# Cross-covariance attention and a mixture of adapters: z and logits in one product, norms of k from products of k with itself

## The chip, the core and the metric

The kernel runs on one core of a Trainium2 chip. A core has TensorE (PE, matrix products, with its weight loads shown as PEld), VectorE (DVE), ScalarE (ACT), GpSimd (POOL) and SyncE (SP, which here only issues transfers), an on-chip memory of 128 partitions, a smaller memory that products are written to (PSUM, in banks of 2 KB for each partition), and 16 DMA engines that the queues of SP, ACT and POOL share. The metric is the device time of one execution in microseconds (us), the median over runs.

## The reference

q, k and v are float32 of shape (4, 6400, 256): 4 batches of 6400 rows and 256 channels. The output has 25600 rows of 256.

```python
qn = q / (norm(q, axis=1) + 1e-06)            # norms over the 6400 rows, for each channel
kn = k / (norm(k, axis=1) + 1e-06)
s = kn.transpose(0, 2, 1) @ qn / tau          # 256 x 256 for each batch
a = exp(s - s.max(-1)); a /= a.sum(-1) + 1e-09
x = v @ a                                     # 6400 x 256 for each batch
logits = x @ w_gate                           # 8 experts
# the two largest of 8 are kept, their softmax is w; for each kept expert e of a row:
out = x + sum_e w_e * ((x @ A[e]) @ B[e])     # A[e] is 256 x 16, B[e] is 16 x 256
```

## The kernel before

Rows are dealt so that a partition holds 50 consecutive rows of a batch. A *chunk* is one row from each partition, 128 rows; a batch has 50 chunks, or 25 *pairs*. A *unit* is two pairs (the last of a batch is one pair).

**Loads.** GpSimd's queue loads q, k and v and casts them to bf16 on the way (`load_more`). q and k share a tile of 10 chunks, with 4 such buffers; v comes in tiles of 18, 16 and 16 chunks, with 3 buffers. The first 4 chunks of q and k come in float32 over SP's queue into a staging tile and are cast by VectorE and ScalarE, and SP also loads the three small weights `ast`, `wst`, `bst`. The order of the loads is a list sorted by due times, moved by `LEAD`.

**First half of a batch.** `gram` (L331) adds k^T q over the 50 chunks in the bank `acc`. `square` (L308 on VectorE, L311 on ScalarE) squares pieces of up to 4 chunks of q and k, `add_squares` (L320, VectorE) adds halves of a piece, and `norm` (L345) sums over partitions by products with a column of ones into `nrm`. Then comes a chain of small steps `chain0` to `chain6`: logarithm and exponential for the root (L357, L359), reciprocal, the scaling of `acc` (L375), a product that spreads the q norms over partitions (L384), the exponential with its row sums (L396), transposes (L409) and products of the transposed matrix with `w_gate` (L426) and A (L428), which give `wa_sb`: 8 columns for the logits and 128 for z, so that v alone is multiplied.

**Second half.** For each unit, `transposes` (L493) turns v around on TensorE and ScalarE or VectorE copies it out (L500, L503). `logits` (L521) makes the logits of 10 pairs in one bank; `gating` copies them (L546) and works out the gates in a dozen small VectorE operations (L551 to L592). `z_gz` (L625) makes z in one of two banks (four at the end) and VectorE gates it directly from there into `gz` (L629). `gz_t` (L641) transposes gz into the same bank, a copy gives `gzT` (L646, L649). `y_mm` (L658) makes v a, `delta` (L667) adds gzT times B in the same bank, and ScalarE (L679, few by VectorE) copies the sum into the tile `ys`, of which there are 7, each for 5 pairs. A full tile goes out over ScalarE's queue (`send`, L694); the last 5 pairs go out one by one over SP's queue (L684).

**What sets the order.** The program is written out by a planner in the kernel's own Python: a loop `while nd < NPT` keeps an estimated clock for each engine and for the DMA, lists what TensorE could do next (Gram, norm, transposes, logits, z, gz transposes, y, delta, the chain) with the time at which it could begin, and takes the first that is ready by a fixed order of preference. The other engines' instructions are written out at the same time. The estimates shape only the order; each engine then runs its instructions in that order and waits for what they need. Stores are held back while the planner thinks that the DMA has more than `BACKLOG` us to do, unless too few `ys` tiles are left. Batch 0's small constants are built by VectorE (`constants`) and TensorE (`constant_a`, L275) at chunks 16 and 30 of the first Gram matrix.

Of the kernel before, what the change touches and what calls it, by code (L numbers as in the profile page):

```python
# [8 lines left out]
FP32 = mybir.dt.float32  # L9
# [7 lines left out]
def kernel(  # L17
# [30 lines left out]
    GATE = 10  # L48
# [4 lines left out]
    YB = 7  # L53
    VTB = 10
    FIRST = 4
    LEAD = [0.0, 0.1, -0.2, 0.2]
    BACKLOG = 4.0
# [3 lines left out]
    if VT[-1] > 10:  # L61
        V_PARTS[B - 1, len(VT) - 1] = [VT[-1] - 6, 6]
# [58 lines left out]
    sq_pool = ctx.enter_context(tc.tile_pool(name="sqp", bufs=4))  # L121
    s2_pool = ctx.enter_context(tc.tile_pool(name="s2p", bufs=4))
# [5 lines left out]
    work = ctx.enter_context(tc.tile_pool(name="work", bufs=3))  # L128
    ps_acc = ctx.enter_context(tc.tile_pool(name="psacc", bufs=1, space=bass.MemoryType.PSUM))
# [29 lines left out]
    def load_more(limit=1000):  # L159

        while limit and loads:
            pick = None
            for x in loads[:6]:
                kind = x[1]
                if x[0] > loads[0][0] + 0.25:
                    break
# [13 lines left out]
            left[kind].append(3 * size if kind == "qk" else size)  # L180
# [43 lines left out]
    transfer("store", 2 * FIRST * CHUNK + 0.5, 1.9)  # L224
# [18 lines left out]
    load_more(3)  # L243

# [41 lines left out]
    for b in range(B):  # L286
        pieces[b] = []
        for i, n in enumerate(QKT):
            sizes = ([FIRST] if (b, i) == (0, 0) else []) + (FIRST_PARTS.get(i, [n]) if b == 0 else [n])
            o = qk_c0[i]  # L290
            for m in sizes:
                for w in range(2):
                    pieces[b] += [(w, o + x, min(4, m - x)) for x in range(0, m, 4)]
                o += m

# [27 lines left out]
    squared, added = [], []  # L323

    def gram(b, c):
        if c == 0:
            acc[b] = ps_acc.tile([P, CC, C], FP32, tag="acc", name="acc")
        s, o = qk_at[c]
        t = tiles["qk"][b, s]
        for ic in range(CC):  # L330
            nc.tensor.matmul(  # L331
                acc[b][:, ic, :], t[:, 1, o, ic * P:(ic + 1) * P], t[:, 0, o, :],
                start=(c == 0 and ic == 0), stop=(c == NC - 1), skip_group_check=True)
        st.setdefault(b, {})["acc_end"] = end = run("pe", 0.22)
        used("qk", b, c, 1, end)

    def norm():
        b, i, s2, _ = added.pop(0)
        w, c, n = pieces[b][i]
        if i == 0:  # L340
            nrm[b] = ps_nrm.tile([P, 512], FP32, tag="nrm", name="nrm")
        for x in range(n // 2):
            for ic in range(CC):
                j = w * CC + ic
                nc.tensor.matmul(  # L345
                    nrm[b][:, j:j + 1], s2[:, x, ic * P:(ic + 1) * P], ones_bf[:, 0:1],
                    start=(i == 0 and x == 0 and ic == 0), stop=(i >= len(pieces[b]) - 2),
                    skip_group_check=True)
        st.setdefault(b, {})["nrm_end"] = run("pe", 0.035 * n)
        if i == len(pieces[b]) - 1:  # L350
            st[b]["normed"] = NC

    def chain0(b):
        d = st.setdefault(b, {})
        lnn = bat.tile([P, 4], FP32, name="lnn")
        norms = nrm[b][:, 0:4]
        nc.scalar.activation(lnn, norms, ACT.Ln)  # L357
        rt = bat.tile([P, 4], FP32, name="rt")
        nc.scalar.activation(rt, lnn, ACT.Exp, scale=0.5)  # L359
        d["rt"] = rt  # L360
        d["at"] = run("act", 0.4, d["nrm_end"])
# [19 lines left out]
    def chain2(b):  # L381
        d = st[b]
        bc = nrm[b][:, 256:512]
# [5 lines left out]
        d["at"] = run("dve", 0.75, run("pe", 0.45, d["at"]), d["tk_end"])  # L389
# [64 lines left out]
    for b in range(B):  # L454
        f = 0
        for n in [5, 5, 5, 5, 3, 2] if b == B - 1 else [GRP] * (NPAIR // GRP):
            g = {"b": b, "f": b * NPAIR + f, "n": n}
# [4 lines left out]
        while f < NPAIR:  # L462
            n = min(GATE, NPAIR - f)
# [14 lines left out]
    pt_end = [0.0, 0.0]  # L478

    def transposes(u):  # L480
# [25 lines left out]
        r["g"]["vT_end"] = end  # L506
        pt_end.append(end)

    def quicker(act, dve):
        return "act" if clock["act"] + act < clock["dve"] + dve else "dve"  # L510

    def logits(gr):

        n, b = 2 * gr["n"], gr["b"]
        lp = ps_t.tile([P, 512], FP32, tag="pt", name="lp")[:, 0:n * E].rearrange(
            "p (s e) -> p s e", s=n)
        i = 0
        for u in range(gr["u0"], gr["u1"]):
            for sc in range(2 * units[u]["n"]):
                for ic in range(CC):  # L520
                    nc.tensor.matmul(lp[:, i, :], units[u]["vT"][:, ic, sc, :], st[b]["wa"][:, ic, 0:E],  # L521
                                     start=(i == 0 and ic == 0), stop=(i == n - 1 and ic == 1),
                                     skip_group_check=True)
                i += 1
        gr["lp"] = lp
        gr["lp_end"] = run("pe", 0.055 * n, gr["vT_end"])

    def gating(gr):
# [15 lines left out]
        def op_lg():  # L544
            d["lg"] = t3("lg")
            V.tensor_copy(d["lg"], gr["lp"])  # L546
# [359 lines left out]
```

## Time and profile before

| | |
|---|---|
| median of 3 runs | 255.96 us (255.96 to 256.38) |
| the profiled execution | 256.35 us |
| its span, first to last instruction | 254.6 us |
| mean granted TensorE clock | 0.932 |
| busy: PE, DVE, ACT, POOL | 216.3, 169.2, 174.5, 32.3 us |
| read from HBM, written | 78.91 MB, 26.21 MB |

A row of a group names the line, the engine and the operation, what is written and read with its shape, and how often it ran; behind the bar stand its busy time in all and the mean of one in ns, then the time that the engine idled before it and what ended that. Rows of the chain and of the timeline begin with the start and the duration in us. Matrix products overlap, so the mean of one is longer than the distance from one to the next; the chain's rows, which give a run of products and its length, show the distance. For a DMA queue a row gives packets, MB as written, and the share of the 16 engines' time. The window rows give for a stretch the busy time and count of PE, PEld, DVE, ACT and POOL, then the granted clock, the DMA share and the GB/s moved; a DMA share can pass 1, since transfers overlap.

### The profile page before, as it was taken

The numbers are of one execution on the slowest core, as the hardware profiler recorded it, in microseconds if no ns is written. First come the engines' busy times: TensorE is split into PE (matmuls) and PEld (weight loads), VectorE is DVE, ScalarE is ACT, GpSimd is POOL, SyncE is SP. The second block draws the span as 40 slices with busy tenths as digits, with TensorE's granted clock in tenths as the row PEclk, the third lists the DMA queues.
The fourth block names the chain that finished last, engine by engine and source line by source line (L and its number), as shares of the span: only waits on it lengthen the run. The fifth ranks groups of instructions, "written<-read, shape, count | busy, mean of one in ns | idle before, by whom it ended". The sixth has DMA issues, their size and how long they took to land.

```text
span 254.6 us, 6828 instructions
## 1 busy us (share of the span) xinstructions
PE 216.3 (85%) x2872; PEld 189.5 (74%) x2872; DVE 169.2 (66%) x476; ACT 174.5 (69%) x279; POOL 32.3 (13%) x66
## 2 busy tenths in 40 slices
PE   0758977678999999999799946599999999999990
PEld 0445766467999989998699934389899999789980
DVE  1468554546867888788777644738879786967650
ACT  2745666648888999777796566917969866565750
POOL 8031241110111110101101000120001000000000
PEclk9999995587999999999999995779999999999996
DMA  7999999999999999999999999999999999999995
GB/s 211 228 213 216 207 213 216 217 210 218 215 216 217 213 220 208 220 212 253 321 273 264 315 314 267 215 214 213 234 299 290 269 303 320 390 427 419 416 383 220
DMA packets 12558, 66.76 MB, mean 262 GB/s; under 512 B 1520, under 2 KB 2032, under 8 KB 8816
## 3 DMA queue, kind: packets, MB, share of 16 engines
q0 software_dynamic: 8352, 38.80, 74.6%
q10 hardware_dynamic: 2736, 24.90, 23.6%
q1 hardware_dynamic: 1440, 2.63, 3.0%
q8 instruction: 22, 0.36, 0.5%
q14 instruction: 8, 0.07, 0.1%
HBM read 78.91 MB, written 26.21 MB: 413 GB/s over the span
## 4 chain that ended last, share of the span: by engine, by line
DMA 61%; PE 27%; ACT 3%; issue 2%; DVE 2%; POOL 1%; ACTq 1%; DVEq 0%; POOLq 0%
DMA qk<-in_k_dram 50%; DMA vt<-in_v_dram 11%; PE acc L331 8%; PE y_ps L658 7%; PE y_ps L667 3%; PE zg L625 3%; PE vT_ps L493 1%; PE zg L641 1%; PE nrm L345 1%; ACT ys L679 1%; ACTq L694 1%; DVE s L320 1%; POOL qk L191 1%; ACT vT L500 1%; PE A_ps L275 1%
## 5 line engine op out<-in xcount | busy, mean ns | idle before, releaser
L311 ACT ACTIVATE sq<-qk 128x1024 bf16<-128x1024 bf16 (+1 forms) x105 | 89.7, 900 | 22.2 <-DMA qk<-in_k_dram 10.7
L331 PE MATMUL acc<-qk 128*128 128x256 bf16 x400 | 66.8, 321 | 17.1 <-DMA qk<-in_k_dram 10.4
L679 ACT COPY ys<-y_ps 128x512 f32<-128x512 f32 x96 | 54.6, 586 | 20.8 <-PE y_ps L667 20.1
L331 PEld LDWEIGHTS <-qk 128*128 128x128 bf16 x400 | 41.7, 112 | 27.8 <-DMA qk<-in_k_dram 12.2
L658 PE MATMUL y_ps<-a_bf,vT 128*128 128x256 bf16 x400 | 59.3, 274 | 1.0 <-ACT ys L679 1.0
L320 DVE TENSOR_TENSOR s<-sq 128x512 bf16<-128x512 bf16 (+1 forms) x120 | 40.6, 375 | 9.5 <-ACT sq L311 5.7
L629 DVE TENSOR_TENSOR gz<-zg,gate 128x512 bf16<-128x512 f32 (+1 forms) x52 | 34.1, 669 | 15.4 <-PE zg L625 14.9
L658 PEld LDWEIGHTS <-vT 128*128 128x128 bf16 x400 | 36.4, 98 | 5.1 <-issue 1.6
L667 PE MATMUL y_ps<-ball_sb,gzT 128*128 128x256 bf16 x200 | 36.0, 272 | 0.6 <-ACT gzT L646 0.6
L493 PE MATMUL vT_ps<-ident,vt 128*128 128x128 bf16 x400 | 30.5, 224 | 2.2 <-DMA vt<-in_v_dram 1.1
L625 PE MATMUL zg<-wa_sb,vT 128*128 128x128 bf16 x400 | 30.3, 223 | 0.0
L345 PEld LDWEIGHTS <-s 128*128 128x128 bf16 x400 | 21.3, 101 | 12.0 <-DVE s L320 8.3
L500 ACT COPY vT<-vT_ps 128x1024 bf16<-128x1024 bf16 (+1 forms) x19 | 18.5, 991 | 17.0 <-PE vT_ps L493 16.7
L345 PE MATMUL nrm<-ones_bf,s 128*128 128x1 bf16 x400 | 22.9, 166 | 7.9 <-DVE s L320 6.6
L493 PEld LDWEIGHTS <-vt 128*128 128x128 bf16 x400 | 25.4, 100 | 4.0 <-DMA vt<-in_v_dram 3.0
L503 DVE COPY vT<-vT_ps 128x1024 bf16<-128x1024 bf16 (+1 forms) x33 | 21.7, 664 | 8.4 <-PE vT_ps L493 7.9
L625 PEld LDWEIGHTS <-vT 128*128 128x128 bf16 x400 | 25.9, 100 | 0.8
L191 POOL DMA_DIRECT2D qk<-in_q_dram x22 | 12.2, 556 | 94.1 <-ACT sq L311 35.8
L649 DVE COPY gzT<-zg 128x512 bf16<-128x512 bf16 (+1 forms) x40 | 16.4, 415 | 7.2 <-PE zg L641 6.5
L667 PEld LDWEIGHTS <-gzT 128*128 128x128 bf16 x200 | 18.0, 97 | 2.9 <-ACT gzT L646 0.9
L641 PE MATMUL zg<-ident,gz 128*128 128x128 bf16 x200 | 19.5, 219 | 0.7 <-DVE gz L629 0.7
L308 DVE TENSOR_TENSOR sq<-qk 128x1024 bf16<-128x1024 bf16 (+1 forms) x15 | 9.7, 654 | 13.0 <-DMA qk<-in_k_dram 7.0
(65 smaller groups left out, 158.3 us busy)
## 6 DMA issues: line engine op xcount, KB each, us to landing
out_dram<-ys ACTq DMA_DIRECT2D x19, 1280.0 KB, 12.2
qk<-in_q_dram POOLq DMA_DIRECT2D x18, 640.0 KB, 25.7
qk<-in_k_dram POOLq DMA_DIRECT2D x18, 640.0 KB, 27.0
vt<-in_v_dram POOLq DMA_DIRECT2D x7, 1024.0 KB, 30.0
vt<-in_v_dram POOLq DMA_DIRECT2D x3, 1152.0 KB, 33.0
vt<-in_v_dram POOLq DMA_DIRECT2D x2, 640.0 KB, 18.6
out_dram<-ys SPq DMA_DIRECT2D x5, 256.0 KB, 4.6
stage<-in_q_dram SPq DMA_DIRECT2D x1, 512.0 KB, 3.8
```

Of the source, the lines that this page charges most:

```text
L311: nc.scalar.activation(sq, x, ACT.Square)
L320: nc.vector.tensor_tensor(out=s2, in0=sq[:, 0:n, :], in1=sq[:, n:2 * n, :], op=OP.add)
L331: nc.tensor.matmul(acc[b][:, ic, :], t[:, 1, o, ic * P:(ic + 1) * P], t[:, 0, o, :], start=(c == 0 and ic == 0), stop=(c == NC - 1), skip_ ...
L345: nc.tensor.matmul(nrm[b][:, j:j + 1], s2[:, x, ic * P:(ic + 1) * P], ones_bf[:, 0:1], start=(i == 0 and x == 0 and ic == 0), stop=(i >= l ...
L493: nc.tensor.matmul(pt[:, ic, sc, :], vt[:, o, ic * P:(ic + 1) * P], ident, is_transpose=True, start=(i == 0), stop=(i == 2 * nch - 1))
L503: nc.vector.tensor_copy(vT, pt)
L625: nc.tensor.matmul(z[:, sc, :], r["vT"][:, ic, sc, :], st[b]["wa"][:, ic, E:E + ER], start=(sc == 0 and ic == 0), stop=(sc == nch - 1 and ...
L629: nc.vector.tensor_tensor(out=gz.rearrange("p c (e r) -> p c e r", e=E), in0=z.rearrange("p c (e r) -> p c e r", e=E), in1=gr["gate"][:, r ...
L641: nc.tensor.matmul(gt[:, sc, :], r["gz"][:, sc, :], ident, is_transpose=True, start=(sc == 0), stop=(sc == nch - 1))
L658: nc.tensor.matmul(y[:, sc, :], r["vT"][:, ic, 2 * x + sc, :], st[r["b"]]["a"][:, ic, :], start=(sc == 0 and ic == 0), stop=False, skip_gr ...
L667: nc.tensor.matmul(y[:, sc, :], r["gzT"][:, 2 * x + sc, :], ball_sb, start=False, stop=(sc == 1), skip_group_check=True)
L679: nc.scalar.copy(dst, y)
```

## The change

1. **z and logits.** `logits` and `z_gz` are gone. `z_mm` multiplies a unit's transposed v by all 136 columns of `wa_sb` into a pair of banks `zp` and copies the result to an on-chip tile `zs` (ScalarE or VectorE, whichever the planner thinks earlier). `gating` reads the logits there; `gate_z` gates z from there, on VectorE, or on GpSimd once the planner has issued every load. `gz_t` now writes to a bank of its own: the one for transposes of v, or at the end the two of `acc` and `nrm`.
2. **Norms.** `SQ` says which of q (0) and k (1) are still squared. In batch 0 neither is, in batches 1 to 3 only q. For the others `gram` multiplies each block of 128 channels by itself and adds that in `nrm`; `chain0` takes the diagonal with the identity.
3. **Small weights** are loaded over GpSimd's queue behind the first q and k loads, no longer over SP's.
4. **Stores.** The last 5 pairs share a `ys` tile and go out as 3, 1 and 1 pairs. There are 6 `ys` tiles.
5. **The planner**: other gate groups (10, 10, 5 as before for 25 pairs, now written out), other due times and estimates, `BACKLOG` 9 for 4, and another order of preference between z, transposes and the rest.

```diff
-    YB = 7
+    YB = 6
     VTB = 10
+    ZSB = 2
     FIRST = 4
-    LEAD = [0.0, 0.1, -0.2, 0.2]
-    BACKLOG = 4.0
+    GATES = [10, 10, 5]
+    GATE = max(GATES)
+    TAIL = [3, 1, 1]
+    SQ = [(), (0,), (0,), (0,)]
+    LEAD = [0.0, 0.15, 0.2, 0.2]
+    BACKLOG = 9.0
...
-    ps_z = ctx.enter_context(tc.tile_pool(name="psz", bufs=2, space=bass.MemoryType.PSUM))
+    ps_z = ctx.enter_context(tc.tile_pool(name="psz", bufs=1, space=bass.MemoryType.PSUM))
...
-    nc.sync.dma_start(ast, moe_A.rearrange("e (g j) r -> (e g) j r", j=2 * E))
-    nc.sync.dma_start(wst, moe_w_gate.rearrange("(p cc) e -> p (cc e)", p=P))
-    nc.sync.dma_start(bst, moe_B.rearrange("e r d -> (e r) d"))
...
     make_identity(nc, ident_f)
     load_more(3)
+    nc.gpsimd.dma_start(wst, moe_w_gate.rearrange("(p cc) e -> p (cc e)", p=P))
+    nc.gpsimd.dma_start(bst, moe_B.rearrange("e r d -> (e r) d"))
+    nc.gpsimd.dma_start(ast, moe_A.rearrange("e (g j) r -> (e g) j r", j=2 * E))
...
     def gram(b, c):
...
-        for ic in range(CC):
-            nc.tensor.matmul(
-                acc[b][:, ic, :], t[:, 1, o, ic * P:(ic + 1) * P], t[:, 0, o, :],
-                start=(c == 0 and ic == 0), stop=(c == NC - 1), skip_group_check=True)
+        for j in range(2 * CC):
+            w, ic = divmod(j, CC)
+            x = t[:, w, o, ic * P:(ic + 1) * P]
+            if w not in SQ[b]:
+                nc.tensor.matmul(nrm[b][:, j, :], x, x, start=b not in begun,
+                                 stop=(c == NC - 1), skip_group_check=True)
+                begun.add(b)
+            if w == 1:
+                nc.tensor.matmul(acc[b][:, ic, :], x, t[:, 0, o, :], start=(c == 0 and ic == 0),
+                                 stop=(c == NC - 1), skip_group_check=True)
...
     def chain0(b):
...
+            nc.vector.tensor_tensor(out=own[:, 0:n, :], in0=nrm[b][:, j:j + n, :],
+                                    in1=ident_f.unsqueeze(1).to_broadcast([P, n, P]), op=OP.mult)
+            nc.vector.tensor_reduce(out=ss[:, j:j + n], in_=own[:, 0:n, :], axis=AX.X, op=OP.add)
...
+    def z_mm(u):
...
+        zp = ps_z.tile([P, 2, 512], FP32, tag="zp", name="zp")
+        for x in range(r["n"]):
+            z = zp[:, x, 0:2 * (E + ER)].rearrange("p (s d) -> p s d", s=2)
+            for sc in range(2):
+                for ic in range(CC):
+                    nc.tensor.matmul(z[:, sc, :], r["vT"][:, ic, 2 * x + sc, :], st[b]["wa"][:, ic, :],
+                                     start=(sc == 0 and ic == 0), stop=(sc == 1 and ic == 1),
+                                     skip_group_check=True)
...
+        if quicker(0.16 + 0.114 * nch, 0.14 + 0.142 * nch) == "act":
+            nc.scalar.copy(dst, src)
...
+            nc.vector.tensor_copy(dst, src)
...
+    def gate_z(u):
...
+        eng = "pool" if 1 and not loads else "dve"
+        (nc.gpsimd if eng == "pool" else nc.vector).tensor_tensor(
             out=gz.rearrange("p c (e r) -> p c e r", e=E),
...
-        gt = r["zg"].bitcast(BF16)[:, 0:512].rearrange("p (s d) -> p s d", s=4)[:, 0:nch, :]
+        if free_from[0] is None:
+            full = ps_t.tile([P, 512], FP32, tag="pt", name="gzT_ps")
+        elif u % 2:
+            full = ps_acc.tile([P, 512], FP32, tag="acc", name="gzT_ps")
+        else:
+            full = ps_nrm.tile([P, 512], FP32, tag="nrm", name="gzT_ps")
...
+        eng = nc.sync if gr["f"] >= NPT - GRP else nc.scalar
+        eng.dma_start(out_v[gr["b"], :, c0:c0 + n, :], gr["blk"]["ys"][:, w:w + n, :])
```

More of the change, by code (lines that the diff above doesn't have):

```diff
@@ L291 @@
             for m in sizes:
-                for w in range(2):
+                for w in SQ[b]:
                     pieces[b] += [(w, o + x, min(4, m - x)) for x in range(0, m, 4)]
                 o += m
+    squared, added = [], []
     def piece_lands(b, i):
@@ L321, in add_squares, with norm @@
         added.append((b, i, s2, run("dve", 0.12 + 0.13 * n, end)))
-    squared, added = [], []
+    begun = set()
+    def norm():
+        b, i, s2, _ = added.pop(0)
+        w, c, n = pieces[b][i]
+        if b not in nrm:
+            nrm[b] = ps_nrm.tile([P, 2 * CC, P], FP32, tag="nrm", name="nrm")
+        for x in range(n // 2):
+            for ic in range(CC):
+                nc.tensor.matmul(
+                    nrm[b][:, w * CC + ic, 0:1], s2[:, x, ic * P:(ic + 1) * P], ones_bf[:, 0:1],
+                    start=b not in begun, stop=(c + n == NC and x == n // 2 - 1), skip_group_check=True)
+                begun.add(b)
+        st.setdefault(b, {})["nrm_end"] = run("pe", 0.035 * n)
+        if i == len(pieces[b]) - 1:
+            st[b]["normed"] = True
     def gram(b, c):
@@ L335, in gram @@
-        used("qk", b, c, 1, end)
[L337 to L351, printed above, removed]
@@ L461 @@
         f = 0
[L462 to L463 removed]
+        for n in GATES:
             g = {"b": b, "f": b * NPAIR + f, "n": n, "ready": False, "u0": len(units)}
@@ L505, in transposes @@
         r["vT"], r["vT_end"] = vT, end
-        r["g"]["vT_end"] = end
         pt_end.append(end)
[L509 to L526, printed above, removed]
     def gating(gr):
@@ L791 @@
                      [pt_end[-2], min(clock["act"], clock["dve"]) - slack])
-            t_cand = (at if ok else 1e9, "t")
-            pairs.insert(len(pairs) if nt - nz >= AHEAD_T else max(0, len(pairs) - 1), t_cand)
+            more.append((at if ok else 1e9, "t"))
+        gated = sum(u < NU and units[u]["g"]["ready"] for u in range(ng, ng + 3))
+        pairs = more + pairs if gated < 3 else pairs + more
         g_cand = []
         if added:
+            b = added[0][0]
             at = added[0][3]
-            if added[0][1] == 0 and added[0][0] > 0 and chain_at[added[0][0] - 1] < 3:
-                at = 1e9
+            if b and b not in begun:
+                at = max(at, st[b - 1].get("bc_end", 1e9))
             g_cand.append((at, "norm"))
```

225 lines of the change are left out of this document (122 added, 103 removed).

## The prediction

> **What bounds the kernel now.** I read the page first, then the DMA queues in two stretches of 10 us, then the windows at both ends, and last the chain in order of time. The page gives the load of the queues and the busiest engine:
>
> ```profile
> span 254.6 us, 6828 instructions
> PE 216.3 (85%) x2872; PEld 189.5 (74%) x2872; DVE 169.2 (66%) x476; ACT 174.5 (69%) x279; POOL 32.3 (13%) x66
> ...
> q0 software_dynamic: 8352, 38.80, 74.6%
> q10 hardware_dynamic: 2736, 24.90, 23.6%
> q1 hardware_dynamic: 1440, 2.63, 3.0%
> ```
>
> The DMA view of 70 to 80 us (loads alone) and of 230 to 240 us (stores alone) gives the rate of each kind:
>
> ```profile
> q0 software_dynamic: 464, 2.12, 104.4%
> ...
> q10 hardware_dynamic: 461, 4.20, 99.7%
> ```
>
> Loads count as bf16 here, which is half of what is read. At 2.12 MB in 10 us the 38.80 MB take 183.0 us; at 4.20 MB the 24.90 MB of stores take 59.3 us and SP's 2.63 MB 6.3 us. Together 248.6 us of transfers in a span of 254.6. The windows show where the other 6 us are (columns: stretch, length, then busy us and count of PE, PEld, DVE, ACT, POOL; granted clock, DMA share, GB/s):
>
> ```profile
> 0.00:1.00 1.00, 0.00 (x0) 0.00 (x0) 0.19 (x3) 0.26 (x1) 0.21 (x4) 1.00 0.00 0
> 1.00:2.00 1.00, 0.00 (x0) 0.00 (x0) 0.04 (x2) 1.00 (x1) 0.76 (x2) 1.00 0.40 45
> 2.00:3.00 1.00, 0.00 (x0) 0.00 (x0) 0.00 (x0) 0.02 (x1) 1.00 (x3) 1.00 0.65 172
> ...
> 45.00:50.00 5.00, 2.75 (x16) 1.97 (x17) 3.20 (x10) 3.60 (x5) 0.98 (x2) 0.50 1.06 220
> ...
> 150.00:155.00 5.00, 0.77 (x11) 0.58 (x12) 1.02 (x4) 1.34 (x3) 0.00 (x0) 0.67 1.02 320
> ...
> 240.00:245.00 5.00, 5.00 (x60) 4.62 (x59) 2.79 (x7) 2.88 (x6) 0.00 (x0) 1.00 0.90 374
> 245.00:250.00 5.00, 2.99 (x30) 2.23 (x27) 1.45 (x4) 2.58 (x5) 0.00 (x0) 1.00 0.97 395
> 250.00:254.60 4.60, 0.00 (x0) 0.00 (x0) 0.00 (x0) 0.00 (x0) 0.00 (x0) 0.57 0.43 163
> 252.00:253.00 1.00, 0.00 (x0) 0.00 (x0) 0.00 (x0) 0.00 (x0) 0.00 (x0) 0.50 0.28 109
> ```
>
> The first 3 us move 0.22 MB, worth 0.5 us: 2.5 us are lost there. 2.5 + 248.6 = 251.1, and the wire runs dry near 252.6. So the wire is the bound, and at most 252.6 - 251.1 = 1.5 us can be won on it. The same comes from the rows of the end: 374 and 395 GB/s beside 420 cost 0.55 + 0.30 us, and the slow drain after 250 us some 0.6. TensorE is no bound before the end: it idles in 150 to 155 us. But behind the last Gram matrix it sets the pace, so both nearly meet:
>
> ```profile
> 28.32 1.73 PE A_ps L275 x16
> ...
> 168.94 26.33 DMA qk<-in_k_dram
> ...
> 197.36 0.46 PE acc L331 x4
> ...
> 199.81 0.08 PE nrm L345 x4
> ...
> 205.04 0.45 PE vT_ps L493 x8
> 205.48 0.49 PE nrm L384 x2
> ...
> 214.75 1.00 PE lp L521 x40
> ...
> 227.03 0.45 PE zg L625 x8
> 227.48 0.44 PE y_ps L658 x4
> ...
> 228.57 0.22 PE zg L641 x4
> ...
> 229.68 0.44 PE y_ps L667 x4
> ...
> 248.23 0.23 PE y_ps L667 x2
> 248.49 0.59 ACT ys L679
> ```
>
> From the last Gram product (197.8) to the last delta (248.5) are 50.7 us; from there to the end of the span 6.1 (copy, SP's issue, landing, the program's end).
>
> **The change part by part.** *TensorE.* By these rows one logits product costs 25 ns, one norm product 20, one of 128 columns 56, one of 256 columns 110. Removed: 400 x 25 = 10.0 us of logits, 250 x 20 = 5.0 of norms. Added: 500 products of q or k with itself, 500 x 56 = 28.0, and 8 more columns on 400 z products, 1.4. Net +14.4 us, but not at the end. The order of the instructions puts behind the last Gram product, before: 100 transposes of v, 144 z, 100 logits, 76 gz transposes, 156 y, 80 deltas, 16 norms and the chain, 47.2 us, which took 50.7 (1.07 each). After: 100, 100 (at 59 ns), none, 64, 156, 80 and the chain: 41.6 us, with 1.07 44.6. This end gets 6 us shorter.
>
> *In front of it.* From the weights `wa` of batch 0 to the last Gram product the sum of the same counts rises from 123.6 to 133.7 us. Before, that stretch ran from 44.9 to 197.8 us with waits for data in it, such as the two windows above. After, it starts later, see below, and at 1.07 needs 143 us: from 50 to 54 that is 193 to 197. The data bound (the last k landed at 195.3) stands where it stood, since the loads behind it are the same; one y buffer less (6 for 7) makes one block of 1.31 MB go out earlier, 3.1 us on the wire ahead of it. I take the last Gram at 195 to 201, 198 for the sum, so TensorE ends at 198 + 44.6 = 242.6 where 248.5 would still be harmless.
>
> *Weights by GpSimd's queue.* The three small loads leave SP and stand behind eight q and k loads; each issue waits for an earlier landing, as POOL's rows do:
>
> ```profile
> 16.76 0.54 POOL L192 DMA_DIRECT2D qk<-in_k_dram  x1 [1.49 <-DMA qk<-in_k_dram]
> ...
> 192.38 1.06 POOL L195 DMA_DIRECT2D vt<-in_v_dram  x2 [12.02 <-PE y_ps L667]
> ```
>
> Ahead of them go 72 chunks of 65.5 KB, 4.7 MB at 212 GB/s = 22.3 us, and the staged 1 MB, 2.5: they land at about 28.5 us. VectorE then builds the constants (8 x 0.35 us and some 1.4 of small ones), so that `A_ps`, at 28.32 before, comes near 33 to 35, with 20 chunks of Gram and norm products (8.9 us, up to twice that at the clock of 0.50 that idling brought at 45 us) behind it on the same queue. Price: 6 to 10 us of delay in batch 0. It is hidden by the 57 us that TensorE does not work before the last Gram (197.8 less 141.0 of counted work) and by the loads queued: those that need no tile of these 20 chunks are 2 x 70 chunks of q and k and 34 of v, 11.4 MB, 54 us of wire, so that the next ones are wanted at about 58 us, while the tiles come free at 40 to 47. If that cover is gone it costs its full length, the second rival. The rest of the start is bounded by -0.3 us (less on SP's queue beside the staged chunks) and +0.3 us.
>
> *ScalarE and VectorE.* These rows are by shape:
>
> ```profile
> L311 ACT ACTIVATE sq<-qk 128x1024 bf16<-128x1024 bf16 x67 | 69.2, 1056 | 18.7 <-DMA qk<-in_k_dram 10.7 <-DMA qk<-in_q_dram 5.0 <-DVE s L320 3.0
> L679 ACT COPY ys<-y_ps 128x512 f32<-128x512 f32 x96 | 54.6, 586 | 20.8 <-PE y_ps L667 20.1
> ...
> L629 DVE TENSOR_TENSOR gz<-zg,gate 128x512 bf16<-128x512 f32 x48 | 32.5, 689 | 14.5 <-PE zg L625 13.9
> L320 DVE TENSOR_TENSOR s<-sq 128x512 bf16<-128x512 bf16 x80 | 31.8, 419 | 7.8 <-ACT sq L311 5.3 <-PE nrm L345 2.2
> ...
> L576 DVE TENSOR_TENSOR e<-lm,m 128x160 f32<-128x160 f32 (+1 forms) x12 | 3.5, 291 | 0.0
> ...
> masks.py:199 POOL TENSOR_SCALAR_AFFINE_SELECT ident<-ident 128x128 bf16<-128x128 bf16 x1 | 0.3, 289 | 0.1
> ```
>
> ScalarE loses 39 large squares (41 us) and more small ones, and gains 33 copies of z at about 0.62 us (by the y copy, 544 for 512 elements): 20 us, so it ends lighter. VectorE loses 50 large sums (21 us), 21 gatings (14 us) and the logits' copies and gains 19 z copies of about 0.73 us. Neither is a bound, 0 us. The diagonal of the norm products adds three small VectorE operations to each chain, some 1.2 us; in return the chain no longer waits for squares: before, 7.7 us lay between the last Gram and the chain's product (205.48); now about 3. I count 0 for it, -4 to +1.2 as ends, since other work fills TensorE meanwhile.
>
> *Gating by GpSimd.* All 21 products stand behind the last load issue (192.4 us), so no load waits for them. No run shows such a product on GpSimd; VectorE's 0.69 us is the lower bound, four times the select on 128 elements, 1.16 us, the nearest row of that engine, and twice that for its two inputs, 2.3, the upper. I take 1.16: 24 us in about 50, while TensorE has 3.6 us of work for each. 0 us; at 2.3, 48 us, it would be the bound. The Trainium skill, GPSIMD Engine Reference, "Performance versus the Vector engine", puts a two-input operation there at about 2.6 cycles of 1.2 GHz an element, which is an estimate of 1.1 us for 512; the sum would be the same by it.
>
> *Stores.* The same bytes; the last 5 pairs leave as 3, 1, 1 instead of five. The last piece is one pair as before: 0 us.
>
> **Sum.** Nothing is taken off the wire. TensorE's end moves from 248.5 to about 242.6, so the stores stand queued to the end, and the wire runs dry about 1.1 us sooner (of the 1.5; the ends are 0 and 1.5). The span goes from 254.6 to 253.5. The profiled execution took 256.35 us, 1.75 more than its span, and lies 0.39 above the median of 255.96; so the median comes to 253.5 + 1.75 - 0.39 = 254.9, rounded to 255.0.
>
> **Rivals.** *Nothing moves the end.* The wire bounds and the drain stays as it is: 255.5 to 256.4. For it: 248.6 us of transfers are untouched. Against it: 374 GB/s at 240 us.
> *Slower: TensorE falls behind from batch 0.* The place is `A_ps` behind the weights, the price 6 to 10 us and 14.4 us of added products. It decides once the last Gram comes after 248.5 - 44.6 = 203.9. With 209 TensorE ends at 253.6: span 259.7, median 261.1; just beyond the point it is 256.5. Middle 258.5. For it: 85% busy. Against: the idle window at 150 us.
> *Slower: VectorE and GpSimd shut each other out.* Seven of the twelve gating operations of a group read two on-chip tiles, 0.29 us each. If each waits out a GpSimd product of 1.16, a group's gates come 8.1 us late; if it meets one half the time and waits half of it, 2 us. TensorE has 5.4 us of other work there. Two groups of batch 3 can lose up to 10 us together: TensorE ends at 252.6, median 260.1, and from 6 us on it decides; 258 is its middle. The Trainium skill speaks for this one: SBUF — State Buffer, "Who interferes with whom", says that a VectorE instruction with two SBUF inputs contends with a GpSimd instruction that reads SBUF, and that the loser blocks for the whole instruction; no run here shows it yet.
> *The wire runs dry while loading.* A later free tile leaves a gap of 1 to 3 us: 257 to 259. Against it: where I put the releases in the order beside the bytes ahead of each later load, 13 us or more of wire are left, an estimate by the counts above.
>
> **How the numbers follow.** This kernel's runs differ by 0.2%, so I call 0.2% (0.5 us) a change. Chances: forecast 0.42 (254.4 to 255.4), nothing moves 0.19, TensorE behind 0.20, shut out 0.11, dry wire 0.08. Faster: the forecast and a hundredth or two of the next, 0.43; same: the rest of it and the mild ends of the others, 0.20; slower 0.37. The range runs from 254.3 to 259.5 and leaves out half of the case of a late TensorE and the ends of the other slow ones, some 0.18; the likeliest one's own range is 254.4 to 255.4.
>
> **What would show it.** Right: DMA share near 1.0 with about 420 GB/s up to 250 us, the last delta before 247, ScalarE under 150 us busy, GpSimd products of about 1.2 us, `A_ps` near 34 us. Wrong: a last Gram after 204 us, a window with a DMA share under 0.9 before 235, or gating operations on VectorE far above 0.29 us beside GpSimd's products.

## The result, and the profile after

The changed kernel takes 256.76 us in the median (255.97 to 257.69 over 22 runs), the kernel before 256.19 (255.94 to 256.41) beside it. The ratio is 1.0025, its 95% interval 1.0017 to 1.0034: slower by a quarter of a per cent, where 255.0 us, 0.4% faster, was forecast. The profiled execution took 256.51 us, its span is 254.7 (before 254.6). The runs of the changed kernel fall in two groups, fifteen up to 256.87 us and seven from 257.48 on, as do those of two experiments below (half the self-products, no first store); the profiles of these three are all of the lower group, and no view tells what parts the groups.

The page of the changed kernel, engines and queues:

```profile
span 254.7 us, 6368 instructions
PE 216.1 (85%) x2722; PEld 196.1 (77%) x2722; DVE 145.3 (57%) x388; ACT 138.9 (55%) x247; POOL 54.8 (21%) x90
...
q0 software_dynamic: 8480, 39.07, 74.9%
q10 hardware_dynamic: 2736, 24.90, 23.6%
q1 hardware_dynamic: 720, 2.36, 2.6%
```

ScalarE is 36 us lighter and VectorE 24, in the direction announced, and the transfers are as large as before. The span did not move. Windows at the end:

```profile
230.00:235.00 5.00, 4.96 (x63) 4.50 (x61) 3.46 (x12) 4.08 (x10) 2.15 (x3) 1.00 1.00 419
235.00:240.00 5.00, 4.17 (x45) 3.69 (x44) 4.69 (x15) 3.28 (x8) 2.98 (x3) 1.00 0.92 385
240.00:245.00 5.00, 5.00 (x53) 4.48 (x51) 1.55 (x4) 3.47 (x7) 2.65 (x3) 1.00 0.82 339
245.00:250.00 5.00, 3.97 (x34) 2.98 (x32) 1.18 (x3) 2.50 (x5) 0.00 (x0) 1.00 0.84 346
```

The wire is full to 235 us and then short: 385, 339 and 346 GB/s, where before had 422, 374 and 395. TensorE's end no longer hides behind queued stores. Its rows in the timeline, last Gram product and last delta, first after, then before:

```profile
203.17 0.27 PE L367 MATMUL acc<-qk 128*128 128x256 bf16 x1
...
249.39 0.38 PE L692 MATMUL y_ps<-ball_sb,gzT 128*128 128x256 bf16 x2
```

```profile
197.22 0.60 PE L331 MATMUL acc<-qk 128*128 128x256 bf16 x4
...
248.07 0.38 PE L667 MATMUL y_ps<-ball_sb,gzT 128*128 128x256 bf16 x2
```

They end at 203.4 and 249.8 us, before at 197.8 and 248.4. The stretch between them, called the *tail* from here on, is shorter (46.3 us for 50.6), but it begins 5.6 us later. Where that comes from shows in the issue of the last load of k (timeline) and its time to landing (DMA view of that stretch, in us at the end of the row):

```profile
166.29 0.54 POOL L201 DMA_DIRECT2D qk<-in_k_dram  x1
...
qk<-in_k_dram POOLq DMA_DIRECT2D x1, 640.0 KB, 33.4
```

It is issued at 166.3 us, 2.6 sooner than before, and lands at 199.7, 4.4 later. The DMA view from the start to that landing gives what went over the wire, and how many blocks of 1.31 MB (1280 KB) had been issued; first after, to 199.7 us, then before, to 195.3:

```profile
q0 software_dynamic: 7955, 36.26, 88.7%
q10 hardware_dynamic: 1138, 10.44, 12.8%
...
out_dram<-ys ACTq DMA_DIRECT2D x8, 1280.0 KB, 11.4
```

```profile
q0 software_dynamic: 7823, 35.96, 90.2%
q10 hardware_dynamic: 930, 8.54, 10.7%
...
out_dram<-ys ACTq DMA_DIRECT2D x7, 1280.0 KB, 12.2
```

The loads are the same: of 36.26 MB, where 35.96 stood before, the three small weights are 0.27, which came over SP's queue before. The stores are 1.90 MB more, with one block more issued. At the stores' 420 GB/s that is 4.5 us, the whole delay. On a full wire this sum has to come out, whichever of the two moved the other; that the stores move the load is shown by the experiments, in the kernel before by the number of `ys` tiles and in the changed one by the store left out.

### The profile page after: what moved, and what is told of

It is laid out like the page before. It is cut to its first block, busy times and chain, and to the rows that moved or that the text cites. A ratio compares the mean times of both kernels' runs of the same rounds, so it can differ in the third digit from the quotient of the medians.

```text
span 254.7 us, 6368 instructions
## 1 busy us (share of the span) xinstructions
PE 216.1 (85%) x2722; PEld 196.1 (77%) x2722; DVE 145.3 (57%) x388; ACT 138.9 (55%) x247; POOL 54.8 (21%) x90
## 4 chain that ended last, share of the span: by engine, by line
PE 46%; DMA 39%; DVE 9%; ACT 2%; issue 1%; POOL 0%; DVEq 0%; POOLq 0%
DMA qk<-in_k_dram 31%; PE y_ps L683 10%; PE acc L367 9%; DMA bst<-in_moe_B_dram 8%; PE nrm L363 6%; PE zp L626 6%; PE y_ps L692 5%; PE vT_ps L526 4%; PE gzT_ps L664 2%; DVE ys L702 1%; ACT vT L533 1%; DVE lm L569 1%; PE nrm L413 1%; DVE a_wide L278 1%; PE nrm L344 1%
## 5 line engine op out<-in xcount | busy, mean ns | idle before, releaser
L363 PE MATMUL nrm<-qk 128*128 128x128 bf16 x500 | 79.3, 226 | 11.7 <-DMA qk<-in_k_dram 5.2
L367 PE MATMUL acc<-qk 128*128 128x256 bf16 x400 | 80.9, 280 | 0.0
L705 ACT COPY ys<-y_ps 128x512 f32<-128x512 f32 x94 | 54.0, 588 | 15.8 <-PE y_ps L692 14.8
L363 PEld LDWEIGHTS <-qk 128*128 128x128 bf16 x500 | 48.3, 102 | 13.7 <-DMA qk<-in_k_dram 6.0
L367 PEld LDWEIGHTS <-qk 128*128 128x128 bf16 x400 | 40.2, 100 | 4.6 <-issue 0.4
L323 ACT ACTIVATE sq<-qk 128x1024 bf16<-128x1024 bf16 (+1 forms) x41 | 37.3, 928 | 1.0 <-DVE s L332 0.9
L626 PE MATMUL zp<-wa_sb,vT 128*128 128x136 bf16 x400 | 32.8, 224 | 5.4 <-ACT zs L633 3.7
L633 ACT COPY zs<-zp 128x544 f32<-128x544 f32 (+1 forms) x33 | 19.7, 598 | 15.0 <-PE zp L626 14.8
L645 POOL TENSOR_TENSOR gz<-zs,gate 128x512 bf16<-128x512 f32 (+1 forms) x21 | 20.9, 1017 | 31.6 <-DVE gate L602 21.9
L672 DVE COPY gzT<-gzT_ps 128x512 bf16<-128x512 bf16 (+1 forms) x39 | 15.9, 409 | 10.4 <-PE gzT_ps L664 10.0
L636 DVE COPY zs<-zp 128x544 f32<-128x544 f32 (+1 forms) x19 | 13.2, 693 | 14.5 <-PE zp L626 14.5
L645 DVE TENSOR_TENSOR gz<-zs,gate 128x512 bf16<-128x512 f32 (+1 forms) x31 | 19.5, 668 | 0.2
```

What stands on the lines that cost most here:

```text
L323: nc.scalar.activation(sq, x, ACT.Square)
L363: nc.tensor.matmul(nrm[b][:, j, :], x, x, start=b not in begun, stop=(c == NC - 1), skip_group_check=True)
L367: nc.tensor.matmul(acc[b][:, ic, :], x, t[:, 0, o, :], start=(c == 0 and ic == 0), stop=(c == NC - 1), skip_group_check=True)
L626: nc.tensor.matmul(z[:, sc, :], r["vT"][:, ic, 2 * x + sc, :], st[b]["wa"][:, ic, :], start=(sc == 0 and ic == 0), stop=(sc == 1 and ic == 1),
L633: nc.scalar.copy(dst, src)
L645: (nc.gpsimd if eng == "pool" else nc.vector).tensor_tensor(out=gz.rearrange("p c (e r) -> p c e r", e=E), in0=gr["zs"][:, r["w"]:r["w"] + ...
```

## The experiments

All ratios are to the kernel before, with 95% intervals. In the expectations A is the reading that early stores delay the last k load, B that VectorE and GpSimd shut each other out, C that batch 0 starts late, D that TensorE's added products are too much, E that the missing `ys` tile is at fault; S is A in the six runs made last. Some edits change only an engine, a queue or leave something out, and every queue keeps its order. Others make the planner write another order; they turned out to be a class of their own.

**Edits that keep the order**

*GpSimd's products back on VectorE.*

```diff
-        (nc.gpsimd if eng == "pool" else nc.vector).tensor_tensor(
+        nc.vector.tensor_tensor(
```

> The changed kernel with the 21 late products of z and gate on VectorE; every other engine keeps its order. Theory A (the last k lands later, at 199.7 us, because one more block of stores goes ahead of it, and TensorE's work behind it sets the end): the gating operations at 235 to 238 us take 0.24 us again in place of 0.65 to 1.0, the last delta comes about 1 us sooner, time 255.8 to 256.5, ratio to the kernel before 0.999 to 1.001. Theory B (VectorE and GpSimd shutting each other out is the whole loss): the wire stays full to the end, time 255.0, ratio 0.995. Theory C (the late weights of batch 0): no change, ratio 1.0025.

257.65 us, 1.0066 (1.0048 to 1.0084): slower than the changed kernel (the intervals don't overlap), so GpSimd's part is a gain of about 0.4%, and all expectations were too low. Its windows show VectorE nearly full where it had room with GpSimd (3.46 us busy from 230 to 235 us in the changed kernel):

```profile
225.00:230.00 5.00, 4.97 (x68) 4.54 (x66) 5.00 (x11) 3.00 (x5) 0.00 (x0) 1.00 1.02 430
230.00:235.00 5.00, 4.37 (x53) 3.77 (x51) 4.76 (x16) 2.64 (x7) 0.00 (x0) 1.00 0.88 368
```

But the time isn't lost there: the tail, from 204.2 to 250.5 us, takes the same 46.3 us. The profiled execution loses its 0.8 us ahead of the last Gram product, although the last k lands sooner (198.4 us), and what delays TensorE there was not found.

*The weights back on SP's queue*, at the place they had before (three `nc.gpsimd.dma_start` become `nc.sync.dma_start`).

> The changed kernel with the three small weights loaded over SP's queue at the start, as before; the order on TensorE is the same. Theory A: the product of the weights comes at about 27 us in place of 32.4, the last k still lands at 199 to 200 us, time as the changed kernel within 0.5 us, ratio 1.001 to 1.004. Theory B: the same. Theory C: the delay of batch 0 is what shifts the end, time 255.0 to 255.5, ratio 0.996.

256.94 us, 1.0039 (1.0027 to 1.0051). `A_ps` begins at 27.8 us for 32.4, yet the last Gram product ends at 203.6 and the last delta at 249.9: no better. Batch 0 is not the cause; C falls.

*Every GpSimd product made twice.*

```diff
+        for _ in range(2 if eng == "pool" else 1):
             (nc.gpsimd if eng == "pool" else nc.vector).tensor_tensor(
```

> The changed kernel with each of the 21 GpSimd products done twice into the same tile (the same result), which doubles their time and the time that they can shut VectorE out. If that matters at the end: the two-input gating operations on VectorE beside them stay at 0.65 to 1.0 us and more of them are hit, the last delta comes 2 to 6 us later, ratio 1.010 to 1.025. If TensorE has other work for the wait: ratio below 1.006.

269.90 us, 1.0531 (1.0514 to 1.0549), beyond what either reading expected. In its waits (engine, line, what was waited for: us in all, times, longest) GpSimd now tops TensorE's list, and between 235 and 240 us the wire carries 63 GB/s:

```profile
PE gzT_ps L665 <- POOL gz L646: 7.0, 11, 1.1
...
235.00:240.00 5.00, 4.00 (x46) 3.25 (x47) 4.13 (x8) 1.00 (x4) 4.47 (x5) 1.00 0.15 63
```

So at twice 1.06 us a product GpSimd holds the end back, as the prediction had said of 2.3 us; at 1.06 it doesn't. How much of this is GpSimd's own time, and how much the time for which it holds VectorE up (last section), this run doesn't part.

**Edits that let the planner rewrite the order**

First the changed kernel. *A block is sent only when one tile more is waiting* (`> YB - 2` becomes `> YB - 1`):

> The changed kernel, but the planner sends a store only when 6 y tiles are unsent, not 5, so that one block of 1.31 MB (3.1 us) less goes out ahead of the last k. Theory A: the last k lands at 196 to 197 us in place of 199.7 and the last delta comes near 247, time 255.2 to 255.8, ratio 0.996 to 0.999. Theories B and C: the last delta stays near 249.7, ratio 1.0025. Against all: with no y tile to spare TensorE may wait for stores, and the planner's order changes throughout, which may cost 1 us.

264.38 us, 1.0302 (1.0264 to 1.0341). The last k lands at 189.9, 10 us sooner, but the last Gram product comes only at 201.3, and the tail is 54.8 us.

*Batch 3's loads with an earlier due time* (`LEAD[3]` 0.4 and 0.6 for 0.2):

> The changed kernel with the due times of batch 3's q and k 0.2 of a batch earlier, so that its last q and k tiles go ahead of a v tile of batch 2. Theory A (the moment at which the last k lands, and TensorE's work behind it, set the end): the last k lands at 195 to 197 us in place of 199.7, the last Gram product ends at 199 to 201 in place of 203.4, the last delta near 247, time 255.2 to 256.0, ratio 0.996 to 0.999. Theory D (TensorE's 14 us of added work leave it no slack anywhere, whatever lands when): the last delta stays at 249 to 251, ratio 1.002 to 1.006.

263.66 us, 1.0296 (1.0281 to 1.0311). The last load of k still went out at 166.5, since its tile waits for a Gram product; last Gram 206.6.

> The same with 0.4 of a batch: all q and k of batch 3 go ahead of the last v tile of batch 2. Theory A: the last k lands at 190 to 193 us, time 254.8 to 255.6, ratio 0.995 to 0.998, unless TensorE runs out of transposed v while it waits, which would show as idle time on v. Theory D: ratio 1.002 to 1.006.

266.97 us, 1.0430 (1.0391 to 1.0468). Here the last k landed at 192.7 and the last Gram product came at 200.3, yet the last delta at 261.9: the tail is 61.6 us. The landing alone doesn't set the end; the work left behind counts as much.

*Gate groups of 6* (`GATES = [6, 6, 6, 6, 1]`), and the same with 7 `ys` tiles, for which the smaller `zs` makes room:

> The changed kernel with gate groups of 6, 6, 6, 6 and 1 pairs in place of 10, 10 and 5: the control of the next run. Twelve small VectorE operations for each of 8 more groups, some 20 us of VectorE, which has about 110 us free. Theory E (the missing y tile, by the stores that it forces ahead of the loads, is what eats the gain): the last Gram product still ends at 202 to 205 us, ratio 1.000 to 1.008.

265.76 us, 1.0301 (1.0246 to 1.0356), last Gram 213.7.

> The same with 7 y tiles, for which the smaller groups leave room: the first store goes out after 24 copies of y, not 19. Theory E: the last Gram product ends 3 to 5 us sooner than in the run with 6 tiles, the wire stays full past 240 us, time 254.8 to 255.8, ratio 0.995 to 0.999, some 0.7% under the control. Theory D (TensorE's added work is the whole cause, tiles or not): as the control within 0.2%.

263.78 us, 1.0312 (1.0271 to 1.0354), last Gram 209.8. The tile brought the last Gram 4 us forward, but the ratios don't differ: inconclusive.

*q and k squared in all batches, no self-products* (`SQ = [(0, 1)] * 4`):

> The changed kernel with the norms of q and k from squares throughout, as before: TensorE does 23 us less, ScalarE and VectorE get 64 and 75 pieces back. Theory D: TensorE's last delta comes 3 us or more sooner than 249.8, time under 255.5, ratio below 0.998. Theory E with ScalarE and VectorE as the engines that the products relieved: 257 to 260, ratio 1.004 to 1.015.

269.41 us, 1.0528 (1.0480 to 1.0576); ScalarE busy 183 us, VectorE 180, last Gram 212.1.

*7 `ys` tiles, room made by 5 tiles of transposed v for 10* (`YB = 7`, `VTB = 5`):

> The changed kernel with 7 y tiles as before, their place taken from the transposed v (5 tiles for 10); the planner rewrites the order. Theory S: last Gram 199 to 201, last delta 245.5 to 248, 0.988 to 0.997. If the rewritten order matters more, as in each earlier run that changed it: 1.01 to 1.05.

287.72 us, 1.1216 (1.1171 to 1.1260). In the profiled execution (291.66 us, the longest of the six) the last Gram product came at 195.1, sooner than in any other run, and up to the last delta TensorE then idled 23.4 us, 14.8 of it waiting for gated z. Which of the two pool sizes did that was not told apart.

Then the kernel before. *6 `ys` tiles and `BACKLOG = 9`; each alone; 8 tiles*:

> The kernel before with the stores' rules of the changed one alone: 6 y tiles and a backlog of 9 us. Theory A: a block more goes ahead of the last k, which lands at 198 to 199 us in place of 195.3, the last delta comes at 251 to 252, time 258 to 259.5, ratio 1.008 to 1.013. Theories B and C: nothing of theirs is in this kernel, ratio 0.998 to 1.002.

258.36 us, 1.0086 (1.0073 to 1.0099), last Gram 204.1.

> The kernel before with 6 y tiles in place of 7 and nothing else. If the missing tile is what pushed a block of stores ahead of the last k and made the run with both rules 0.86% slower: ratio 1.006 to 1.010, last k at 198 us or later. If the backlog of 9 us did it: 0.999 to 1.002.

258.55 us, 1.0102 (1.0086 to 1.0117), last Gram 203.3, last delta 251.9.

> The kernel before with a backlog of 9 us in place of 4 and nothing else. If the missing tile did it: ratio 0.999 to 1.002, since the order of the first ten stores is the same as before. If the backlog did it: 1.006 to 1.010.

256.08 us, 1.0003 (0.9994 to 1.0012): `BACKLOG` does nothing here, so the two runs ahead of it come from the sixth tile and the order that the planner writes for it.

> The kernel before with 8 y tiles for 7 (the planner then sends each block later; the order changes). Theory S (stores ahead of the last k load set the last Gram product): one block fewer ahead of it, last k landed near 193, last Gram near 195.5 to 197, last delta near 246 to 248, 0.994 to 0.999; the gain is small since the wire has only 1.5 us to give. If the number of tiles matters only below 7: 0.999 to 1.002.

259.35 us, 1.0124 (1.0100 to 1.0149). The three numbers of tiles side by side, from the DMA views up to the landing and the timelines (us):

| tiles | blocks issued before the last k lands | MB stored by then | last k lands | last Gram | tail | last delta | ratio |
|---|---|---|---|---|---|---|---|
| 6 | 8 | 10.22 | 199.3 | 203.3 | 48.6 | 251.9 | 1.0102 |
| 7 | 7 | 8.54 | 195.3 | 197.8 | 50.6 | 248.4 | 1 |
| 8 | 6 | 7.40 | 192.4 | 197.3 | 55.5 | 252.8 | 1.0124 |

The landing follows the tiles, a block for each, bytes by rate: 1.68 MB more are 4.0 us at 420 GB/s, and it comes 4.0 later; 1.14 MB less are 2.7, and it comes 2.9 sooner. The time doesn't follow them, since the order behind the landing changes too: with 8 tiles the tail is 4.9 us longer, 6.2 of its 55.5 us idle. So the ratio of 1.0102 isn't the price of the tile alone. Of the eleven edits in this part only `BACKLOG` left the time where it was, and the others cost about 1% or more. They show that a last Gram product sooner or later isn't the end by itself, and not what one part of the change is worth.

**Leaving work out, in the changed kernel's own order**

These four were made to part S from D. *Self-products for 26 of 50 chunks* (240 fewer):

```diff
-            if w not in SQ[b]:
+            if w not in SQ[b] and (c % 2 == 1 or c == 0):
```

> The changed kernel with the products of q and k with themselves for 26 of the 50 chunks only (240 products fewer, at 56 ns 13.4 us of TensorE's work; the norms are then too small), every engine's order otherwise the same. Theory S (the stores that stand ahead of the last k load hold the last Gram product back): the last k lands near 199.7 us as in the changed kernel, last Gram product 202 to 203.4, last delta 248.5 to 250, 1.000 to 1.0025 of the time before. Theory D (TensorE's 13.5 us of added work eats the gain): TensorE catches up, last Gram 198 to 200, last delta 245 to 247, 0.988 to 0.994.

*One block not stored, the first or the 17th*:

```diff
-        eng.dma_start(out_v[gr["b"], :, c0:c0 + n, :], gr["blk"]["ys"][:, w:w + n, :])
+        if gr["f"] != 0: eng.dma_start(out_v[gr["b"], :, c0:c0 + n, :], gr["blk"]["ys"][:, w:w + n, :])
```

The other run has `!= 80`.

> The changed kernel without the store of its first block (1.31 MB, 3.1 us of wire, left out of the output), order otherwise the same. Theory S: the last k lands 3 us sooner, near 196.6, last Gram near 200.3, last delta near 247, 0.989 to 0.993 of the time before. Theory D: the data come sooner but TensorE is late anyhow: last Gram at or after 202.5, 0.999 to 1.0025.

> The changed kernel without the store of its 17th block (1.31 MB, issued after the last k load; left out of the output), order otherwise the same: as many bytes fewer as without the first store, but none ahead of the last k. If TensorE's work behind the last Gram product sets the end: last Gram 203.4 and last delta 249.8 as in the changed kernel, 1.000 to 1.0025. If the full wire sets the end (a third theory, W): 3 us sooner, 0.989 to 0.992, like the run without the first store.

*Half the self-products and no first store*:

> Both of the above: self-products for 26 of 50 chunks and no first store, order otherwise the same. Theory S: like the run without the first store alone, 0.988 to 0.993. Theory D: like the run with half the self-products alone, 0.988 to 0.994 (the store gives nothing on top). If both count, the two gains add: last Gram before 197, last delta before 245, 0.980 to 0.986.

The last Gram product and the last delta in the timelines, in the order half the self-products, no first store, no late store, both:

```profile
202.41 0.27 PE L367 MATMUL acc<-qk 128*128 128x256 bf16 x1
...
248.60 0.38 PE L692 MATMUL y_ps<-ball_sb,gzT 128*128 128x256 bf16 x2
```

```profile
200.73 0.27 PE L367 MATMUL acc<-qk 128*128 128x256 bf16 x1
...
246.93 0.38 PE L692 MATMUL y_ps<-ball_sb,gzT 128*128 128x256 bf16 x2
```

```profile
203.32 0.27 PE L367 MATMUL acc<-qk 128*128 128x256 bf16 x1
...
249.52 0.38 PE L692 MATMUL y_ps<-ball_sb,gzT 128*128 128x256 bf16 x2
```

```profile
199.34 0.27 PE L367 MATMUL acc<-qk 128*128 128x256 bf16 x1
...
245.54 0.38 PE L692 MATMUL y_ps<-ball_sb,gzT 128*128 128x256 bf16 x2
```

With the landings from the DMA views (us; "behind" is from the landing to the end of the last Gram product; the ratios are of all runs, the other columns of the profiled execution):

| | last k lands | behind | last Gram | tail | last delta | span | ratio |
|---|---|---|---|---|---|---|---|
| changed kernel | 199.7 | 3.7 | 203.4 | 46.3 | 249.8 | 254.7 | 1.0025 (1.0017 to 1.0034) |
| half the self-products | 199.7 | 3.0 | 202.7 | 46.3 | 249.0 | 254.1 | 1.0005 (0.9983 to 1.0026) |
| no first store | 195.4 | 5.6 | 201.0 | 46.3 | 247.3 | 252.2 | 0.9933 (0.9901 to 0.9965) |
| no 17th store | 199.3 | 4.3 | 203.6 | 46.3 | 249.9 | 254.8 | 1.0045 (1.0032 to 1.0058) |
| both left out | 196.6 | 3.0 | 199.6 | 46.3 | 245.9 | 250.8 | 0.9862 (0.9849 to 0.9874) |

Four things follow. First, the tail is 46.3 us in each, and the span ends 4.9 to 5.1 us behind it: in this order the end is the last Gram product plus a constant. Second, bytes that leave late are free: without the 17th store the wire falls to 204 GB/s between 240 and 245 us and nothing is gained (1.0045, where W had 0.989 to 0.992), so W falls.

```profile
240.00:245.00 5.00, 5.00 (x53) 4.47 (x51) 1.69 (x4) 3.47 (x7) 2.66 (x3) 1.00 0.49 204
```

Third, the same bytes ahead of the last k cost: without the first store it lands 4.3 us sooner, and with half the self-products 3.1 sooner (199.7 to 196.6), which is the 1.31 MB by rate. But in the first of these the last Gram product comes only 2.4 us sooner, because TensorE is not ready for it (5.6 us behind for 3.7). Fourth, halving the self-products alone gains 0.8 us in the profiled executions (the ratios' intervals overlap), since TensorE then waits for the data (0.9 us for k from 190 us on, where it waited 0.2); on top of the store left out it gains 1.4. Both together gain 3.8, where the two apart add up to 3.2; the difference of 0.6 is less than the 1.2 us by which the landings of the two runs without the first store differ, so it shows no more than that the gains add. The sum stays short of what the expectation for both had said: 199.6 and 245.9 for under 197 and 245. So S is the larger part and D the smaller one that stands close behind it; S alone had expected 200.3 and D alone 202.5 for the run without the first store, and 201.0 lies between.

No run beat the kernel before without leaving work out.

## Why the prediction was wrong, by its own steps

*In front of it: this step failed.* "The data bound (the last k landed at 195.3) stands where it stood, since the loads behind it are the same" is false: it moved to 199.7. The step knew of the block that goes out earlier and of its 3.1 us on the wire, put them into the range of 195 to 201, and then took 198 as if they cost nothing. The rows show 1.90 MB, 4.5 us: the block, and by the count of blocks 0.6 MB more of the one issued next (at 188.4 us before, at 189.6 after), of which the later landing let more through. From landing to last Gram it had 2.7 us, and 3.7 came: the timeline has 20 products of k with itself in this stretch, at 56 ns 1.1 us, which the step had not put there; half the self-products give 0.7 back. The step's other bound, TensorE done by 193 to 197, was early too: without the first store the last k landed at 195.4, and TensorE was busy for 5.40 of the 5.60 us up to its last Gram product at 201.0. 4.4 + 1.0 is the miss from 198 to 203.4. That the sixth tile sends that block early follows from the code (`send` goes by `YB - 2`, and in the order of the changed kernel the first store stands behind 21 `ys` copies, before behind 26) and from the kernel before, where a tile less moved the landing by 4.0 us. In the changed kernel itself no run gave the tile back with the order kept.

*TensorE's tail.* Counted work of 41.6 us was right in direction (before 50.6, after 46.3). The factor of 1.07 was too small: 46.3 / 41.6 is 1.11. That is 1.7 us. TensorE idles 2.7 us in it, before 1.6, most of it waiting for the copies of y into `ys` (2.4 us, where before it waited 0.7 for them). The deciding point moves with it: 248.5 - 46.3 = 202.2 in place of 203.9, and the last Gram product passed it by some 1.3 us, which is what the last delta is late (249.8 for 248.4). So the sign of being wrong that the prediction gave, a last Gram after 204 us, was set too late.

*The sum.* It put TensorE's end at 242.6 and let the wire decide. 198 + 44.6 became 203.4 + 46.3, 249.8. No single term did this: the block at its 3.1 us would have given 201 + 44.6 = 245.6, still harmless, but 4.4, 1.0 and 1.7 together used up the 5.9 us between 242.6 and 248.5. The wire is the bound up to 235 us only; the run without a late store shows that behind that point it has room. That "at most 252.6 - 251.1 = 1.5 us can be won on it" was a fair ceiling for a kernel that keeps the wire full to the end, which this one doesn't. That the span grew by only 0.1 us comes from the stretch behind the last delta, 4.9 us for 6.1; the wire is emptier there (346 GB/s for 395 between 245 and 250 us), but that this is the reason is not shown.

*Weights by GpSimd's queue.* Right. `A_ps` began at 32.37 us, a little ahead of the 33 to 35, and moving the loads back gains nothing. The second row is the chain's product, for the next point.

```profile
32.37 1.86 PE A_ps L286 x16
...
206.59 0.70 PE nrm L413 x2
```

*The chain.* Right: its product begins 3.2 us behind the last Gram product, for about 3.

*ScalarE, VectorE.* Right: 138.9 us (under 150), and neither is a bound.

*GpSimd's products.* Their group in the costliest groups has 1059 ns:

```profile
L645 POOL TENSOR_TENSOR gz<-zs,gate 128x512 bf16<-128x512 f32 x19 | 19.7, 1059 | 29.5 <-DVE gate L602 21.9 <-ACT lnn L385 4.3 <-PE gzT_ps L664 3.3
```

That is 1.06 us for 1.16 taken, so the nearest row was a good guide, and the Trainium skill's figure (GPSIMD Engine Reference, "Performance versus the Vector engine", an estimate of 1.1 us) agrees with the row. The price of 0 was too cautious: beside the same order on VectorE it is a gain of about 0.4%.

*The rivals.* "TensorE falls behind" has the outcome, a late last Gram product, but not with its mechanism: the weights cost nothing, and leaving out 13.4 us of self-products, nearly all of the net 14.4 added, brings the end 0.8 us forward, and 1.4 without the first store in the way. "Shut out" happens, as the last section shows, and isn't what sets the end, since without GpSimd the kernel is slower and its tail is as long. "The wire runs dry while loading" didn't come: the share is 1.00 and above in the windows from 30 to 235 us.

*Open.* The profiled spans differ by 0.1 us where the medians differ by 0.57. The account above is of the profiled executions; what spreads the changed kernel's times over 1.7 us, where those before spread over 0.5, is not known.

## What to carry to other kernels

Where loads and stores share a full wire, ask of each buffer given up which store it sends ahead of the last load that anything waits for, and price that store in full, bytes by rate; the same store later can be free. When the work behind the last arrival is a fixed queue, the end is that arrival plus a constant, so write both terms with their errors, and add the errors up, before deciding which bound wins: here three small ones together used up the slack. Where a planner writes the order, test one part with edits that keep the order (another engine, another queue, work left out): edits that let it write a new one cost 1 to 12% here, whatever they were about, but for one of eleven.

## What was not expected of the hardware

VectorE's gating beside GpSimd's products, timeline of the changed kernel, first GpSimd's four products in a row, then VectorE's rows:

```profile
233.87 4.11 POOL L645 TENSOR_TENSOR gz<-zs,gate 128x512 bf16<-128x512 f32 x4
```

```profile
235.10 0.24 DVE L561 TENSOR_REDUCE m<-zs 128x10 f32<-128x80 f32 x1
235.38 0.67 DVE L565 TENSOR_TENSOR e<-zs,m 128x80 f32<-128x80 f32 x1
236.07 0.98 DVE L569 SCALAR_TENSOR_TENSOR lm<-e,zs 128x80 f32<-128x80 f32 x1
237.09 0.24 DVE L574 TENSOR_REDUCE m<-lm 128x10 f32<-128x80 f32 x1
237.36 0.64 DVE L578 TENSOR_TENSOR dm<-m,m 128x10 f32<-128x10 f32 x1
...
238.52 0.24 DVE L589 TENSOR_TENSOR e<-e,e 128x80 f32<-128x80 f32 x1
```

The three operations with two on-chip inputs take 0.64 to 0.98 us, while the last row, behind the products, takes 0.24. They end at 236.05, 237.05 and 238.00, each within 0.12 us behind the end of one of the products (233.87 and multiples of 1.03 give 235.93, 236.95, 237.98). The reduces keep their 0.24. With GpSimd's products on VectorE, the first experiment, the same three operations take 0.24, 0.23 and 0.17:

```profile
236.97 0.24 DVE L565 TENSOR_TENSOR e<-zs,m 128x80 f32<-128x80 f32 x1
...
237.73 0.23 DVE L569 SCALAR_TENSOR_TENSOR lm<-e,zs 128x80 f32<-128x80 f32 x1
...
238.27 0.17 DVE L578 TENSOR_TENSOR dm<-m,m 128x10 f32<-128x10 f32 x1
```

That is the Trainium skill's rule, SBUF — State Buffer, "Who interferes with whom": a VectorE instruction with two SBUF inputs contends with a GpSimd one that reads SBUF, and the loser blocks for the whole instruction; this trace agrees, with these numbers. What surprised is that one small operation with a single input is caught too: `rt`, 128x4, in the chain behind the last Gram product took 0.83 us, from 204.97 to 205.80, beside a product that ends at 205.78. In the kernel before it took 0.16. The rows are GpSimd's and VectorE's of the changed kernel, then VectorE's before:

```profile
204.72 1.06 POOL L645 TENSOR_TENSOR gz<-zs,gate 128x512 bf16<-128x512 f32 x1 [4.34 <-ACT lnn L385]
```

```profile
204.97 0.83 DVE L395 TENSOR_SCALAR rt<-rt 128x4 f32<-128x4 f32 x1
```

```profile
204.22 0.16 DVE L366 TENSOR_SCALAR rt<-rt 128x4 f32<-128x4 f32 x1
```

The same section of the Trainium skill lists that kind of operation, `tensor_scalar`, among those that can take the shared ports, so the two agree here as well. And all of it costs little: without GpSimd's products the tail took the same 46.3 us.
